# One row of running sums, four weight pieces on GpSimd, and a copied k by transfer, in a fused attention, expert and gated kernel

## The chip, the cores and the metric

The kernel runs on one core of a Trainium2 chip. The metric is device time in microseconds of one execution, the median of the runs shown. Engines: PE (TensorE), DVE (VectorE), ACT (ScalarE), POOL (GpSimd), and SP (SyncE), which only issues DMAs here; ACT issues a few as well.

## What is computed

Shapes: B=2, H=8, S=576, D=64 for the attention; 1152 tokens of width 512, four experts of width 1024, then a gated pair of width 1536. All in float32.

```python
scores = scale * np.matmul(q, k.transpose(0, 1, 3, 2))
cum = np.cumsum(np.maximum(s, 0.0), axis=-1)
bias = -(cum[:, :, :, None] - cum[:, :, None, :])
scores = np.where(causal, -1e9, scores + np.minimum(bias, 0.0))
attn = softmax(scores)                 # sum + 1e-9 below
x = attn @ v                           # to (1152, 512)
for e in range(4):
    out += p[:, e:e+1] * (np.maximum(x @ w1[e], 0.0) @ w2[e])
y = ((out @ w_a) * (out @ w_b)) @ w_out
```

For a row of scores the term -cum of the query is the same in every column and drops out of the softmax; what is left to add is cum of the key. The kernel adds it inside the score matmul, as further rows of k against rows of constants of q.

## The kernel before, in words

Attention is worked off in four groups, (batch, query tiles): group 0 is batch 0, tiles 0 to 1; group 1 is batch 0, tiles 2 to 4; group 2 batch 1, tiles 0 to 2; group 3 batch 1, tiles 3 to 4. In each group the eight heads follow each other. One step is one tile of 128 queries of one head, 80 steps in all. `attn_step` (L786) is a software pipeline over them: at step n it transposes the tile of step n-3 on PE, computes the scores of n (`st_scores`, L586), normalizes the tile of n-2 (`st_norm`), takes the softmax of n-1 (`st_softmax`), evacuates the transposes of n-3 (`st_evac`), and after a head's last tile multiplies with v (`st_av`, L660, tile `av`). At a head's first step the next head's k and q are prepared (`prep_job`, L550) and those of the head after that loaded (`load_job`, L537).

Group 0 is in plain float32. Its q, k and v for all heads (`qa`, `ka`, `va`) are loaded at the start. Its score matmul has 67 rows: 64 of head dimension and three rows with a high, middle and low part of cum minus a value `c0` per row, made in `ckr` and copied into `ka` by three DMAs on ACT's queue (L748). GpSimd multiplies q by the scale first (L554). Groups 1 to 3 split every operand into a high part in the rounded float32 format (F32R) and a low part. Their scores are two matmuls: `ks` (high k, and low k in the other 64 rows) against `qh`, and `kb` (high k again, plus the three rows from the DRAM scratch `ckD`) against `qb`. `kb`'s 64 rows are a second copy of high k, made by GpSimd from the raw `kr` (L566); `ks` is made by ACT (L565) and, for its low half, by GpSimd (L569).

The softmax is a fused operation on DVE that adds the mask to the scores and takes the negated row minimum `mn` (L611), an exponential on ACT with its sum `l` (L623), the addition of 1e-9 on ACT (L628), a reciprocal on DVE (L629) and the multiplication on GpSimd (L630).

The first two experts run beside the attention: between the steps PE gets expert matmuls (L258; 576 of 256 columns each belong to the first part). Their weights come in 16 pieces of 512 KB. A piece is loaded by SP into one of three `raw` buffers (L147) and split by `split_piece` (L190) into `wh` and `wl`: the first eight pieces' high half by GpSimd (L214, two operations of 128x512), later ones by ACT (L218), the low half (L219) by GpSimd for odd pieces and DVE for even ones. Products are three matmuls, high times high, high times low and low times high. The tiles `wh` and `wl` share a pool of four buffers with `qa`, `ka`, `va` and `ckr`.

Each engine takes its instructions in order. That order is made beforehand by a list scheduler that models times, from the program's dependences; only the DMAs inside `in_order` keep the order in which they're written. How far the attention steps are spread between expert products is set by `area`, a running sum of the tile widths, and by `ends`, the step at which a group is complete. So a change of one operation can move others far away.

Of the kernel before, what the change touches and what calls it, by code (L numbers as in the profile page):

```python
# [8 lines left out]
F32 = mybir.dt.float32  # L9
# [3 lines left out]
ALU = mybir.AluOpType  # L13
# [32 lines left out]
NTT = NT // P  # L46
NT0 = 256


@with_exitstack  # L50
def fused_kernel(ctx, tc, qT, kT, v, s, dp, w1, w2, wa, wb, wo, out):
# [138 lines left out]
    def split_piece(r, key, form, wide, src, j):  # L190
# [5 lines left out]
        elif form == "half":  # L196
            split(wh, wl, r, nc.gpsimd)
        elif form == "pair" and wide:
            if j == 0:
                wides[key] = pools["cv"].tile([P, NC, 2 * P], I32, tag="tp", name="tp")  # L200
            t = wides[key]
            narrow(t[:, 2 * j : 2 * j + 2], r[:, :, :, 0], r[:, :, :, 1])
            if j:
                split_pair(key, t.bitcast(F32), nc.gpsimd)
        elif form == "pair":
            split_pair(key, r, nc.vector)
        else:
            nsplit[0] += 1
            first_ones = nsplit[0] <= 8
            lo_eng = nc.gpsimd if nsplit[0] % 2 else nc.vector  # L210
            for m in range(2):
                hi = wh[:, 2 * j + m, :]
                if first_ones:
                    nc.gpsimd.tensor_scalar(  # L214
                        out=hi, in0=r[:, m, :], scalar1=1.0, scalar2=1.0, op0=ALU.mult, op1=ALU.mult
                    )
                elif m == 0:
                    nc.scalar.activation(out=wh[:, 2 * j : 2 * j + 2, :], in_=r, func=AF.Copy)  # L218
                lo_eng.tensor_tensor(  # L219
                    out=wl[:, 2 * j + m, :], in0=r[:, m, :], in1=hi.bitcast(F32), op=ALU.subtract  # L220
                )
# [328 lines left out]
    def prep_job(j):  # L550
        j.t = {}
        if j.gi == 0:
            q = first["q"][:, j.h, :]
            nc.gpsimd.tensor_scalar(  # L554
                out=q[:D], in0=q[:D], scalar1=SCALE, scalar2=1.0, op0=ALU.mult, op1=ALU.mult
            )
            j.qh, j.kr, j.vs = q[:RB], first["k"][:RB, j.h, :], first["v"][:, j.h]
            return
# [45 lines left out]
    def st_softmax(j, i):  # L604
# [132 lines left out]
    )  # L737
    for x in (slice(0, NT0), slice(NT0, S)):
        hi, mid, lo = (y[:, x] for y in ck3)
        d_ = dif[:, x]  # L740
        nc.vector.tensor_scalar(out=d_, in0=cum[:, x], scalar1=c0, scalar2=None, op0=ALU.subtract)
        nc.scalar.activation(out=hi, in_=d_, func=AF.Copy)
        nc.vector.tensor_tensor(out=d_, in0=d_, in1=hi.bitcast(F32), op=ALU.subtract)
        nc.scalar.activation(out=mid, in_=d_, func=AF.Copy)
        nc.vector.tensor_tensor(out=lo, in0=d_, in1=mid.bitcast(F32), op=ALU.subtract)
        if x.start == 0:
            for j_ in range(3):
                in_order(nc.scalar.dma_start(  # L748
                    out=first["k"][D + j_ : D + j_ + 1, :, :], in_=ck3[j_][:H, x].bitcast(F32)
                ))  # L750
# [9 lines left out]
    nc.vector.memset(causal, 0.0)  # L760
    nc.gpsimd.affine_select(
        out=causal[:, S - P :], in_=causal[:, S - P :], pattern=[[-1, P]], compare_op=ALU.is_ge, fill=MASKED,
        base=0, channel_multiplier=1,
    )

# [20 lines left out]
    def attn_step():  # L786
# [365 lines left out]
```

## Time and profile before

| | us |
|---|---|
| median of 3 runs | 768.46 (766.67, 768.46, 769.26) |
| the profiled execution | 768.68 |
| its span, first to last instruction | 766.9 |
| PE busy | 721.4 (94%) |
| DVE busy | 534.2 (70%) |
| ACT busy | 334.4 (44%) |
| POOL busy | 440.0 (57%) |

The mean granted clock of PE over the span is 0.984 of full speed. 58.35 MB are moved by DMA. The attention with the first experts takes the first 240 us, about; the rest is matmuls for the experts and the gated pair. The table's shares are means over the span; the stretches are read apart, in the rows below.

### The profile page before, as it was taken

The numbers are of one execution on the slowest core, as the hardware profiler recorded it, in microseconds if no ns is written. First come the engines' busy times: TensorE is split into PE (matmuls) and PEld (weight loads), VectorE is DVE, ScalarE is ACT, GpSimd is POOL, SyncE is SP. The second block draws the span as 40 slices with busy tenths as digits, with TensorE's granted clock in tenths as the row PEclk, the third lists the DMA queues.
The fourth block names the chain that finished last, engine by engine and source line by source line (L and its number), as shares of the span: only waits on it lengthen the run. The fifth ranks groups of instructions, "written<-read, shape, count | busy, mean of one in ns | idle before, by whom it ended". The sixth has DMA issues, their size and how long they took to land.

```text
span 766.9 us, 11091 instructions
## 1 busy us (share of the span) xinstructions
PE 721.4 (94%) x3868; PEld 628.3 (82%) x3868; DVE 534.2 (70%) x1076; ACT 334.4 (44%) x770; POOL 440.0 (57%) x385
## 2 busy tenths in 40 slices
PE   2889989897997999999999999999899999999998
PEld 2559988885986888888888888898698989878886
DVE  5459675757747987676666557669964788888764
ACT  3558766868844433223213232242635424242410
POOL 4979864657731573443123333678466787898600
PEclk9869999999999999999999999999999999999999
DMA  5435411223302030212011111213111222322003
GB/s 164 154 115 203 158 44 53 79 58 109 95 26 83 27 110 29 77 60 75 9 55 56 56 48 62 83 57 107 31 54 56 83 82 83 97 97 82 3 1 124
DMA packets 33208, 58.35 MB, mean 76 GB/s; under 512 B 3104, under 2 KB 18512, under 8 KB 33152
## 3 DMA queue, kind: packets, MB, share of 16 engines
q1 hardware_dynamic: 32944, 57.48, 23.2%
q8 instruction: 31, 0.51, 0.3%
q14 instruction: 25, 0.20, 0.1%
q10 hardware_dynamic: 208, 0.16, 0.1%
HBM read 55.02 MB, written 2.58 MB: 75 GB/s over the span
## 4 chain that ended last, share of the span: by engine, by line
PE 70%; DVE 14%; POOL 6%; ACT 4%; issue 3%; DMA 2%; ACTq 0%; DVEq 0%; POOLq 0%; SPq 0%
PE ps L258 33%; PE psq L258 22%; PE pst L258 6%; PE av L677 4%; POOL wl L72 3%; PE tr L641 2%; PE sc L601 1%; DVE wl L219 1%; PE sc L599 1%; POOL tp L153 1%; PE sc L602 1%; ACT e L623 1%; DVE e L611 1%; POOL ks L569 1%; DMA kr<-in_kT 1%
## 5 line engine op out<-in xcount | busy, mean ns | idle before, releaser
L258 PE MATMUL ps<-wh,h2h 128*128 128x512 f32 x332 | 131.0, 395 | 2.0 <-DVE acc L304 1.7
L72 POOL TENSOR_TENSOR wl<-raw,wh 128x1024 fp32r<-128x1024 f32 x24 | 58.2, 2435 | 124.5 <-ACT wh L71 94.1
L258 PE MATMUL ps<-wl,h2h 128*128 128x512 f32 x332 | 129.7, 391 | 0.0
L258 PE MATMUL ps<-wh,h2l 128*128 128x512 f32 x332 | 125.7, 392 | 0.0
L306 DVE SCALAR_TENSOR_TENSOR acc<-ps,pr,acc 128x512 f32<-128x512 f32 x111 | 82.0, 745 | 38.5 <-PE ps L258 37.6
L258 PE MATMUL psq<-xh,wh 128*128 128x448 f32 (+1 forms) x224 | 81.6, 366 | 1.7 <-DVE xs L699 1.7
L258 PE MATMUL psq<-xl,wh 128*128 128x448 f32 (+1 forms) x224 | 81.6, 364 | 0.0
L258 PE MATMUL psq<-xh,wl 128*128 128x448 f32 (+1 forms) x224 | 81.5, 364 | 0.0
L258 PEld LDWEIGHTS ps<-wh,h2h 128*128 128x128 f32 x332 | 62.4, 188 | 15.0 <-ACT h2h L317 2.0
L258 PEld LDWEIGHTS ps<-wh,h2l 128*128 128x128 f32 x332 | 62.2, 188 | 13.9 <-DVE h2l L72 0.7
L258 PEld LDWEIGHTS ps<-wl,h2h 128*128 128x128 f32 x332 | 62.4, 188 | 11.0
L317 ACT ACTIVATE h2h<-psq 128x448 fp32r<-128x448 f32 (+1 forms) x56 | 29.4, 530 | 94.7 <-PE psq L258 74.6
L630 POOL TENSOR_SCALAR e<-e,r 128x128 f32<-128x128 f32 (+4 forms) x80 | 47.8, 602 | 31.0 <-DVE r L629 27.4
L72 POOL TENSOR_TENSOR wl<-sums,wh 128x1024 fp32r<-128x1024 f32 x24 | 58.5, 2438 | 6.7 <-ACT wh L71 6.7
L611 DVE CUSTOM_DVE_ANT_0 e<-sc,causal 128x128 f32<-128x128 f32 (+3 forms) x80 | 35.9, 452 | 37.8 <-PE tr L641 28.8
L71 ACT ACTIVATE wh<-raw 128x1024 fp32r<-128x1024 f32 x24 | 25.5, 1061 | 69.9 <-PE ps L258 53.7
L258 PE MATMUL psq<-tqh,wh 128*128 128x448 f32 x144 | 53.0, 368 | 1.5 <-DVE h2l L72 1.4
L258 PE MATMUL psq<-tql,wh 128*128 128x448 f32 x144 | 52.6, 365 | 0.0
L623 ACT ACTIVATE e<-e,mn 128x128 f32<-128x128 f32 (+4 forms) x80 | 45.9, 574 | 15.4 <-DVE mn L611 13.5
L258 PE MATMUL psq<-tqh,wl 128*128 128x448 f32 x144 | 52.4, 364 | 0.0
L656 ACT ACTIVATE eh<-tr 128x512 fp32r<-128x512 f32 (+6 forms) x96 | 38.9, 412 | 27.6 <-PE tr L641 26.7
L153 POOL TENSOR_SCALAR tp<-tp 128x512 f32<-128x512 f32 x24 | 47.2, 1983 | 6.1 <-ACT tp L152 6.1
(170 smaller groups left out, 1974.0 us busy)
## 6 DMA issues: line engine op xcount, KB each, us to landing
raw<-in_w SPq DMA_DIRECT2D x40, 512.0 KB, 3.7
raw<-in_wa SPq DMA_DIRECT2D x12, 512.0 KB, 3.6
raw<-in_wb SPq DMA_DIRECT2D x12, 512.0 KB, 3.6
raw<-in_wo SPq DMA_DIRECT2D x12, 512.0 KB, 3.6
kr<-in_kT SPq DMA_DIRECT2D x16, 288.0 KB
vr<-in_v SPq DMA_DIRECT2D x16, 160.0 KB, 3.3
out<-acc SPq DMA_DIRECT2D x9, 256.0 KB, 2.0
qr<-in_qT SPq DMA_DIRECT2D x8, 192.0 KB, 2.6
```

Of the source, the lines that this page charges most:

```text
L71: nc.scalar.activation(out=hi, in_=src, func=AF.Copy)
L72: lo_eng.tensor_tensor(out=lo, in0=src, in1=hi.bitcast(F32), op=ALU.subtract)
L153: nc.gpsimd.tensor_scalar(out=t.bitcast(F32), in0=t.bitcast(F32), scalar1=2.0**-15, scalar2=GMAX, op0=ALU.max, op1=ALU.min,)
L258: nc.tensor.matmul(ps, lhsT=l, rhs=r, start=first and k == 0, stop=last and k == 2, skip_group_check=more)
L306: nc.vector.scalar_tensor_tensor(out=dst, in0=ps, scalar=share, in1=dst, op0=ALU.mult, op1=ALU.add)
L317: nc.scalar.activation(out=hh, in_=src, func=AF.Relu)
L611: nc.vector.tensor_tensor_reduce(out=t.e[:, c0:c1], in0=ps, in1=causal[:, m0 + c0 : m0 + c1], scale=-1.0, scalar=seed, op0=ALU.add, op1=AL ...
L623: nc.scalar.activation(out=t.e, in_=t.e, func=AF.Exp, bias=mn, scale=-1.0, accum_out=t.l)
L630: nc.gpsimd.tensor_scalar(out=t.e, in0=t.e, scalar1=r, scalar2=1.0, op0=ALU.mult, op1=ALU.mult)
L641: nc.tensor.transpose(ps[:, c - c0, :], t.e[:, k0 : k0 + P], ident)
L656: nc.scalar.activation(out=hi, in_=src, func=AF.Copy)
L677: nc.tensor.matmul(ps[:, o:] if j.gi else ps[a : a + D, o:], lhsT=j.vs[:, c, :], rhs=e[:, c, o:], start=(m == 0), stop=(m == len(mms) - 1),)
```

## The change

Group 0 has one row of sums instead of three. q isn't scaled any more: the row of q that meets the sums holds 1/SCALE = 8, the scores come out 8 times too large, and the scale is put into the exponential (L621) and, by a DVE operation on the minimum (L620), into its bias. The running sum is made in two parts, 256 columns first, and the row goes to `ka` by one DMA right after the first part (L734). The high, middle and low rows for the other groups follow over all 576 columns at once. The mask `causal` is made by GpSimd, earlier. In group 0 the 1e-9 is added and the tile normalized by DVE (L629, L633) instead of ACT and GpSimd. Weight pieces: the first NFIRST = 4 have both halves made by GpSimd, the high half in one operation; later ones have the high half made by ACT and the low half alternating as before. The second copy of k becomes a transfer from `ks` to `kb` on SP's queue (L563). `st_av` is called one step later, ahead of `st_evac`; `ends` and `area` follow.

```diff
-            first_ones = nsplit[0] <= 8
-            lo_eng = nc.gpsimd if nsplit[0] % 2 else nc.vector
...
+            lo_eng = nc.gpsimd if nsplit[0] % 2 or nsplit[0] <= NFIRST else nc.vector
+            two = slice(2 * j, 2 * j + 2)
+            if nsplit[0] <= NFIRST:
+                nc.gpsimd.tensor_scalar(
+                    out=wh[:, two, :], in0=r, scalar1=1.0, scalar2=1.0, op0=ALU.mult, op1=ALU.mult
+                )
+            else:
+                nc.scalar.activation(out=wh[:, two, :], in_=r, func=AF.Copy)
...
         if j.gi == 0:
-            q = first["q"][:, j.h, :]
-            nc.gpsimd.tensor_scalar(
-                out=q[:D], in0=q[:D], scalar1=SCALE, scalar2=1.0, op0=ALU.mult, op1=ALU.mult
-            )
-            j.qh, j.kr, j.vs = q[:RB], first["k"][:RB, j.h, :], first["v"][:, j.h]
+            j.qh, j.kr, j.vs = first["q"][: D + 1, j.h, :], first["k"][: D + 1, j.h, :], first["v"][:, j.h]
...
-        nc.gpsimd.tensor_scalar(
-            out=j.kb[:D], in0=j.kr[:D], scalar1=1.0, scalar2=1.0, op0=ALU.mult, op1=ALU.mult
-        )
+        nc.sync.dma_start(out=j.kb[:D].bitcast(F32), in_=j.ks[:D].bitcast(F32))
...
-        nc.scalar.activation(out=t.e, in_=t.e, func=AF.Exp, bias=mn, scale=-1.0, accum_out=t.l)
+        if j.gi == 0:
+
+            nc.vector.tensor_scalar(out=mn, in0=mn, scalar1=SCALE, scalar2=None, op0=ALU.mult)
+        nc.scalar.activation(
+            out=t.e, in_=t.e, func=AF.Exp, bias=mn, scale=-1.0 if j.gi else -SCALE, accum_out=t.l
+        )
...
-        nc.scalar.activation(out=t.l, in_=t.l, func=AF.Copy, bias=1e-9)
+        if j.gi == 0:
+            nc.vector.tensor_scalar(out=t.l, in0=t.l, scalar1=1e-9, scalar2=None, op0=ALU.add)
+        else:
+            nc.scalar.activation(out=t.l, in_=t.l, func=AF.Copy, bias=1e-9)
         nc.vector.reciprocal(out=r, in_=t.l)
-        nc.gpsimd.tensor_scalar(
+        (nc.gpsimd if j.gi else nc.vector).tensor_scalar(
...
+    half = H // 2
+    nc.vector.memset(first["q"][D : D + 1, :half], 1.0 / SCALE)
+
+    nc.vector.tensor_scalar(out=sc[:, :NT0], in0=sc[:, :NT0], scalar1=0.0, scalar2=None, op0=ALU.max)
+    nc.vector.tensor_tensor_scan(
+        out=cum[:, :NT0], data0=ones[:NR, :NT0], data1=sc[:, :NT0], initial=0.0,
+        op0=ALU.mult, op1=ALU.add,
+    )
+    in_order(nc.scalar.dma_start(out=first["k"][D : D + 1, :, :], in_=cum[:H, :NT0]))
...
-        if x := at(n - 3):
-            st_evac(*x)
+        if x := at(n - 4):
             j, i = x
             if i == j.i1 - 1:
                 st_av(j)
+        if x := at(n - 3):
+            st_evac(*x)
...
-    ends = [max(n for n, (j, i) in enumerate(seq) if j.gi == g) + 4 for g in range(len(GROUPS))]
+    ends = [max(n for n, (j, i) in enumerate(seq) if j.gi == g) + 5 for g in range(len(GROUPS))]
...
-    for n in range(len(seq) + 8):
+    for n in range(len(seq) + 12):
```

Three places show how the order of instructions moves. The first is the start of DVE, up to the scan on which the first score matmul waits; `s_sb` holds s, `va` the tile that also holds the sums. Before:

```order
L756 MEMSET qa 3x2048
L722 MEMSET ones 128x576
L758 MEMSET qb_83 3x384
L758 MEMSET qb_84 3x384
L760 MEMSET causal 128x576
L730 TENSOR_SCALAR s_sb<-s_sb 32x576
L731 SCALAR_TENSOR_TENSOR va<-ones,s_sb 32x576
```

Now:

```order
L727 MEMSET qa 1x1024
L725 MEMSET ones 128x576
L742 MEMSET qa 1x1024
L770 MEMSET qb_83 3x384
L770 MEMSET qb_84 3x384
L729 TENSOR_SCALAR s_sb<-s_sb 32x256
L750 TENSOR_SCALAR s_sb<-s_sb 32x320
L730 SCALAR_TENSOR_TENSOR va<-ones,s_sb 32x256
```

The memset of three rows of q became two of one row, that of `causal` left DVE, and the scan comes in a part of 256 columns, behind both halves of the max.

The second is SP's queue where the weights of pieces 4 to 9 are issued (`raw`; names of the others go on with the head, the group's first tile and a number, so `kb_2_2` belongs to head 2 of group 1, whose tiles begin at 2). Before:

```order
L546 DMA qr_1_2_446<-in_qT 128x384
L147 DMA raw<-in_w 128x1024 x2
L546 DMA qr_2_2_503<-in_qT 128x384
L547 DMA kr_1_2_447<-in_kT 128x576
L576 DMA vr_1_2_531<-in_v 128x320
L147 DMA raw<-in_w 128x1024 x2
L548 DMA kb_2_2_505<-ckD 3x576
L547 DMA kr_2_2_504<-in_kT 128x576
L546 DMA qr_3_2_602<-in_qT 128x384
L576 DMA vr_2_2_633<-in_v 128x320
L147 DMA raw<-in_w 128x1024 x2
```

Now:

```order
L149 DMA raw<-in_w 128x1024
L547 DMA qr_1_2_442<-in_qT 128x384
L563 DMA kb_0_2_391<-ks_0_2_435 64x576
L149 DMA raw<-in_w 128x1024
L547 DMA qr_2_2_500<-in_qT 128x384
L548 DMA kr_1_2_443<-in_kT 128x576
L571 DMA vr_1_2_526<-in_v 128x320
L549 DMA kb_2_2_502<-ckD 3x576
L149 DMA raw<-in_w 128x1024
L563 DMA kb_1_2_444<-ks_1_2_493 64x576
L547 DMA qr_3_2_578<-in_qT 128x384
L149 DMA raw<-in_w 128x1024 x3
```

The loads of k's three rows for head 2 (`kb_2_2<-ckD`) stood behind pieces 6 and 7 and now stand ahead of piece 6; the copies `kb<-ks` of heads 0 and 1 are new.

The third is PE at the first scores of head 1 of group 1 (`sc_1_2`, then the tile and a number; L258, now L259, are expert matmuls into `ps`). Before:

```order
L258 MATMUL ps_635<-xl,wh 128x256
L258 MATMUL ps_635<-xh,wl 128x256
L258 MATMUL ps_671<-xl,wh 128x256
L258 MATMUL ps_671<-xh,wl 128x256
L601 MATMUL sc_1_2_2_612<-ks_1_2_496,qh_1_2_445 128x320
L602 MATMUL sc_1_2_2_612<-kb_1_2_448,qb_83 128x320
L677 MATMUL av_6_0_525<-eh_6_0_486,va 64x256
L677 MATMUL av_6_0_525<-eh_6_0_486,va 64x128
L601 MATMUL sc_1_2_3_657<-ks_1_2_496,qh_1_2_445 128x448
L602 MATMUL sc_1_2_3_657<-kb_1_2_448,qb_83 128x448
L641 MATMUL tr_7_0_0_533<-ident,e_7_0_0_481 128x128
```

Now:

```order
L259 MATMUL ps_802<-xh,wl 128x256
L259 MATMUL ps_845<-xh,wl 128x256
L259 MATMUL ps_924<-xh,wl 128x256
L259 MATMUL ps_924<-xh,wh 128x256
L259 MATMUL ps_924<-xl,wh 128x256
L259 MATMUL ps_924<-xh,wl 128x256
L596 MATMUL sc_1_2_2_588<-ks_1_2_493,qh_1_2_441 128x320
L597 MATMUL sc_1_2_2_588<-kb_1_2_444,qb_83 128x320
L596 MATMUL sc_1_2_3_637<-ks_1_2_493,qh_1_2_441 128x448
L597 MATMUL sc_1_2_3_637<-kb_1_2_444,qb_83 128x448
```

What stood after 27 expert matmuls and ahead of the last `av` of group 0 now stands after 84 of them and behind that `av`. Counted over the whole order, 68 expert matmuls stood ahead of the end of the `av` of head 0 of group 1, and now 140; from the end of the `av` of head 4 of group 1 to that of head 1 of group 2 there were 101, and now 18. Near the attention's end, in heads 5 and 6 of group 3, the next head's transposes now stand ahead of the `av`, where they stood behind it.

## Rows read from the trace of the kernel before

**Rows 1.** The page: PE's granted clock in 40 slices.

```profile
PEclk9869999999999999999999999999999999999999
```

**Rows 2.** Waits of PE, 0 to 60 us: engine, line, releaser, total us, times, longest.

```profile
PE sc L599 <- DMA ka<-ckr: 13.4, 1, 13.4
```

**Rows 3.** Chain that ended last, 0 to 16 us: start, length, what.

```profile
1.29 1.76 DVE qa L756
...
5.72 1.36 DVE va L731
...
9.23 0.88 ACTq L748
...
10.97 2.15 DMA ka<-ckr
...
13.42 1.64 PE sc L599 x4
```

**Rows 4.** Timeline of DVE at the start: start, length, engine, line, operation.

```profile
3.24 0.54 DVE L722 MEMSET ones<- 128x576 f32 x1 [0.18 <-issue]
...
3.89 0.78 DVE L758 MEMSET qb<- 3x384 f32 x2
...
5.30 0.38 DVE L730 TENSOR_SCALAR s_sb<-s_sb 32x576 f32<-32x576 f32 x1
...
7.41 0.84 DVE L741 TENSOR_SCALAR dif<-va,c 32x256 f32<-32x256 f32 x2
```

**Rows 5.** Windows of the first group: us, busy PE, PEld, DVE, ACT, POOL; PEclk.

```profile
20.00:30.00 10.00, 9.28 (x37) 5.87 (x35) 5.70 (x15) 6.12 (x24) 9.92 (x17) 1.00 0.45 153
30.00:40.00 10.00, 7.18 (x26) 5.09 (x26) 4.95 (x18) 5.08 (x18) 9.90 (x15) 0.65 0.35 117
...
33.00:48.00 15.00, 13.31 (x42) 8.56 (x42) 5.14 (x18) 6.62 (x25) 14.33 (x20) 0.50 0.25 93
```

**Rows 6.** Windows of three other stretches, same columns.

```profile
52.00:60.00 8.00, 6.17 (x40) 4.98 (x40) 6.37 (x19) 6.53 (x21) 5.20 (x7) 1.00 0.61 200
130.00:135.00 5.00, 4.00 (x32) 3.47 (x30) 3.49 (x13) 4.52 (x16) 4.28 (x8) 1.00 0.26 75
130.00:145.00 15.00, 12.45 (x88) 10.44 (x87) 11.52 (x47) 13.84 (x53) 11.90 (x22) 1.00 0.31 90
```

**Rows 7.** Window at the end of the attention, same columns.

```profile
220.00:240.00 20.00, 14.17 (x90) 11.62 (x89) 10.39 (x26) 9.46 (x24) 4.40 (x6) 1.00 0.07 21
```

**Rows 8.** DVE by form, 18 to 36 us: line, operation, shapes, count, total, mean ns.

```profile
L629 DVE RECIPROCAL r<-l 128x1 f32<-128x1 f32 x10 | 1.4, 155 | 2.7 <-ACT l L628 2.7
```

**Rows 9.** Timeline of DVE beside GpSimd's weight pieces.

```profile
18.41 0.58 DVE L771 TENSOR_SCALAR den<-den 128x9 f32<-128x9 f32 x1 [0.86 <-POOL den L770]
19.38 0.19 DVE L772 RECIPROCAL den<-den 128x9 f32<-128x9 f32 x1
...
26.98 2.01 DVE L219 TENSOR_TENSOR wl<-raw,wh 128x512 fp32r<-128x512 f32 x2
...
42.99 0.42 DVE L611 CUSTOM_DVE_ANT_0 e<-sc,causal 128x256 f32<-128x256 f32 x1 [1.91 <-PE tr L641]
```

**Rows 10.** Chain of the wait for k, 180 to 194 us.

```profile
184.18 3.04 DMA kr<-in_kT
...
187.37 0.61 POOL kb L566
```

**Rows 11.** Chain of two heads near the attention's end.

```profile
228.14 1.16 PE av L677 x8
229.30 0.47 PE tr L641 x4
...
231.28 0.49 ACT eh L656
...
231.80 0.70 DVE el L658
...
232.55 1.16 PE av L677 x8
```

More of the change, by code (lines that the diff above doesn't have):

```diff
@@ L47 @@
 NT0 = 256
+NFIRST = 4
 @with_exitstack
@@ L208, in split_piece @@
             nsplit[0] += 1
-            first_ones = nsplit[0] <= 8
-            lo_eng = nc.gpsimd if nsplit[0] % 2 else nc.vector
-            for m in range(2):
-                hi = wh[:, 2 * j + m, :]
-                if first_ones:
-                    nc.gpsimd.tensor_scalar(
-                        out=hi, in0=r[:, m, :], scalar1=1.0, scalar2=1.0, op0=ALU.mult, op1=ALU.mult
-                    )
-                elif m == 0:
-                    nc.scalar.activation(out=wh[:, 2 * j : 2 * j + 2, :], in_=r, func=AF.Copy)
+            lo_eng = nc.gpsimd if nsplit[0] % 2 or nsplit[0] <= NFIRST else nc.vector
[6 more added lines that the diff above has]
+                nc.scalar.activation(out=wh[:, two, :], in_=r, func=AF.Copy)
+            for m in (2 * j, 2 * j + 1):
                 lo_eng.tensor_tensor(
-                    out=wl[:, 2 * j + m, :], in0=r[:, m, :], in1=hi.bitcast(F32), op=ALU.subtract
+                    out=wl[:, m, :], in0=r[:, m - 2 * j, :], in1=wh[:, m, :].bitcast(F32), op=ALU.subtract
                 )
@@ L565, in prep_job @@
         nc.scalar.activation(out=j.ks, in_=j.kr, func=AF.Copy)
-        nc.gpsimd.tensor_scalar(
-            out=j.kb[:D], in0=j.kr[:D], scalar1=1.0, scalar2=1.0, op0=ALU.mult, op1=ALU.mult
-        )
+        nc.sync.dma_start(out=j.kb[:D].bitcast(F32), in_=j.ks[:D].bitcast(F32))
         nc.gpsimd.tensor_tensor(
@@ L722, in fused_kernel @@
     nc.vector.memset(ones, 1.0)
+    half = H // 2
[6 more added lines that the diff above has]
+    in_order(nc.scalar.dma_start(out=first["k"][D : D + 1, :, :], in_=cum[:H, :NT0]))
+    nc.gpsimd.memset(causal, 0.0)
+    nc.gpsimd.affine_select(
+        out=causal[:, S - P :], in_=causal[:, S - P :], pattern=[[-1, P]], compare_op=ALU.is_ge, fill=MASKED,
+        base=0, channel_multiplier=1,
+    )
+    make_identity(nc, ident)
+    nc.vector.memset(first["q"][D : D + 1, half:], 1.0 / SCALE)
     nc.gpsimd.memset(pick, 1.0)
@@ L729, in fused_kernel @@
         )
-    nc.vector.tensor_scalar(out=sc, in0=sc, scalar1=0.0, scalar2=None, op0=ALU.max)
+    nc.vector.tensor_scalar(out=sc[:, NT0:], in0=sc[:, NT0:], scalar1=0.0, scalar2=None, op0=ALU.max)
     nc.vector.tensor_tensor_scan(
-        out=cum, data0=ones[:NR], data1=sc, initial=0.0, op0=ALU.mult, op1=ALU.add
+        out=cum[:, NT0:], data0=ones[:NR, NT0:], data1=sc[:, NT0:], initial=cum[:, NT0 - 1 : NT0],
+        op0=ALU.mult, op1=ALU.add,
     )
@@ L737, in fused_kernel @@
     )
[L738 to L750, printed above, removed]
+    hi, mid, lo = ck3
+    nc.vector.tensor_scalar(out=dif, in0=cum, scalar1=c0, scalar2=None, op0=ALU.subtract)
+    nc.scalar.activation(out=hi, in_=dif, func=AF.Copy)
+    nc.vector.tensor_tensor(out=dif, in0=dif, in1=hi.bitcast(F32), op=ALU.subtract)
+    nc.scalar.activation(out=mid, in_=dif, func=AF.Copy)
+    nc.vector.tensor_tensor(out=lo, in0=dif, in1=mid.bitcast(F32), op=ALU.subtract)
     for j_ in range(3):
@@ L754, in fused_kernel @@
         ))
-    make_identity(nc, ident)
-    nc.vector.memset(first["q"][D:RB], 1.0)
     for qb in qbs:
         nc.vector.memset(qb[D:].bitcast(F32), 1.0)
[L760 to L764, printed above, removed]
     nc.sync.dma_start(out=pr, in_=dp)
```

1 line of the change is left out of this document (removed).

## The prediction

> **What bounds the kernel now.** I read the page first: the granted clock of PE is at nine tenths or more in 38 of 40 slices, with a dip in the second and third [rows 1]. The run that was profiled took 768.68 us, 0.22 above the median of 768.46; the sum below starts from 768.68. From about 60 us PE is busy nearly all the time, apart from the attention's last third, so the change can only gain where PE stands still. I then looked for those places with PE's waits and with windows. The largest is the start: PE waits 13.4 us, once, for the rows of sums in `ka` [rows 2]. The chain shows how these come about: a memset, the scan, two differences and roundings, the issue of a DMA on ACT's queue, 2.15 us until it lands, then the first scores at 13.42 [rows 3]. The second is 52 to 60 us, where PE is busy 6.17 of 8.00 us [rows 6]. The third are heads with few expert products between their steps: 12.45 of 15.00 us busy, and 4.00 of 5.00 in the emptiest part [rows 6]. The last is the attention's end, 14.17 of 20.00 [rows 7].
>
> **The start: minus 4.2 us.** Three roundings, two subtractions and two of three issues leave the path; the first scores need one scan of 256 columns. DVE begins at 1.29 [rows 3]. It now does two memsets of 1024 columns, half of the 1.76 each [rows 3], and those of `ones` (0.54) and `qb` (0.78) [rows 4]: 0.88 + 0.54 + 0.88 + 0.78 = 3.08. With some 0.4 of gaps, as between the same rows before, that ends at 4.8. Both halves of the max stand ahead of the scan; one of 576 columns took 0.38 [rows 4], and I put 0.5 for two. The scan of 256 takes 256/576 of 1.36, so 0.60. That is 5.9. One issue (0.88) and the landing (2.15) follow [rows 3], then 0.30 from the landing to the first matmul (13.42 less 10.97 and 2.15). The sum is 9.2 instead of 13.42. q's scaling on GpSimd leaves too; it was ahead of its need. The memset of `causal` moves from DVE to GpSimd, which is idle then.
>
> **DVE in the first group: 0, and up to plus 14.3.** Each of 16 steps gives DVE three operations that other engines did or that weren't there: 32 of one column (the minimum times SCALE, the sum plus 1e-9) and 16 that norm a tile. The one-column reciprocal has a mean of 0.155 [rows 8], so 32 x 0.155 = 5.0; a norm costs at most what the subtraction of `dif` costs, 0.84 for two [rows 4], so 16 x 0.42 = 6.7. Away go the low halves of pieces 2 and 4, about 2.0 us each [rows 9]: plus 7.7 in all. DVE was busy 5.70 and 4.95 of 10 us [rows 5], and the group lasts from 13.42 to the last of its tiles at 42.99 [rows 9], so of these 30 us DVE had 9.35 / 20 x 30 = 14.0 free. 6.3 stay free, and PE, which is the busier one there, hides the work. What isn't known is whether DVE is held up by GpSimd, which is busy 9.92 of 10 us with weights [rows 5]. The nearest row says it can be: `den`, nine columns, took 0.58 [rows 9] where a one-column operation takes 0.155, so 0.43 more; its reciprocal, a moment later, took 0.19 [rows 9]. All 48 held like that are 20.6 us, 14.3 more than the room. I take none, since ten reciprocals in the same stretch were not held [rows 8], and keep both ends. The Trainium skill has a rule that speaks against this change: in "SBUF — State Buffer", section "Who interferes with whom", a DVE tensor_scalar may take the port pair that it shares with GpSimd, and then whoever comes second is blocked for the other's whole instruction. By that rule norms and the new one-source operations could all be held, and the sum would be that of the first rival below; the reciprocal isn't on its list, and the trace agrees with both, with one row for each.
>
> **Weights and the lead at 45 to 60 us: minus 1.8.** GpSimd loses 16 norms, 8 scalings of q and four high halves to others, and gives its time to pieces 1 to 4. With the first group done earlier, PE's order has 140 expert matmuls ahead of the end of the next head's `av`, where it had 68. They fill what is idle between 52 and 60, 8.00 - 6.17 = 1.83 [rows 6]. Against that, SP issues the sixth piece only behind `kb_2_2`, which waits for PE's scores of head 0, where it used to issue two pieces ahead of it; so piece 6 is late if anything is. And ACT now does the high halves of pieces 5 to 8, ahead of softmax steps. The bounds are minus 1.8 and, if two pieces come late by a low half of 2.0 each [rows 9], plus 4.0.
>
> **Heads with little expert work: plus 2.6.** The products put forward are missing later. From the `av` of head 4 in the second group to that of head 1 in the third, the order had 101 expert matmuls and now has 18. Three more heads have next to nothing between their steps; such a head takes 4.4 us, from one `av` at 228.14 to the next at 232.55 [rows 11], so three take 13.2. At the emptiest rate, 1.00 idle of 5.00 [rows 6], that is 13.2 / 5 x 1.00 = 2.6. The bounds are 2.2 by the 15-us row (2.55 / 15 x 13.2) [rows 6] and 3.8 by the end of the attention (5.83 / 20 x 13.2) [rows 7].
>
> **The copy of k: minus 0.6.** 24 copies leave GpSimd and become 24 transfers on SP's queue. Most are hidden on either side, as k is prepared a head ahead. In the wait for k, GpSimd's 0.61 stands behind a transfer of `kr` [rows 10]; that one goes. The new transfer starts once ACT has made `ks`, and takes at least the 2.15 of the small one [rows 3] and about the 3.04 of `kr` [rows 10]; a head lasts 4.4 us [rows 11], so it is hidden. Queued behind it on SP are the next `qr`, `kr` and a weight piece, each by the issue of one DMA; bounds minus 1.2 and plus 1.
>
> **av a step later: minus 2.2.** Near the end a head runs as transposes 0.47, evacuation 0.49, low part 0.70, `av` 1.16, one after the other [rows 11]. The changed order puts the next head's transposes ahead of this `av` for two heads, so that `av` runs beside the evacuation: 2 x 1.1. The bounds are 0, if evacuation sets the pace, and minus 2.3.
>
> **The sum**: 768.68 - 4.2 - 1.8 + 2.6 - 0.6 - 2.2 = 762.5. Its own range is 760 to 767: down, what the last three terms still allow (0.4, 0.6 and 0.1, with as much for the start); up, the two largest bounds that don't hang together, 2.2 for `av` and some of the weights' 5.8, not all of it.
>
> **Rivals.** *DVE is held in the first group* (slower). If three quarters of the 48 operations wait as `den` did, 36 x 0.43 = 15.5, less the 6.3 of room, 9.2 come on top: 771.7. All 48 give 776.8. The room is used up at 15 held operations, and from 29 on the kernel is slower than before, (6.2 + 6.3) / 0.43. For it: `den` [rows 9]. Against it: ten reciprocals that weren't held [rows 8]; GpSimd begins on weights only behind DVE's `den`, half-way through the group, and PE isn't waiting for DVE then. 0.17. *The gain is given back*: the sixth piece comes late, so the lead costs half of a low half, 1.0, instead of giving 1.8, heads without expert work cost 3.8 and `av` gives nothing: 768.68 - 4.2 + 1.0 + 3.8 - 0.6 = 768.7, no change. For it: SP's order, and the emptiness of [rows 7]. 0.22. *The clock*: from 33 to 48 us PE was granted 0.50, half of 2.4 GHz, and was busy 13.31 of 15 [rows 5]. If such a stretch lasts half as long again, 7.5 x 0.5 x 13.31 / 15 = 3.3 come on top: 765.8. 0.08. If there is no such stretch, up to 13.31 / 2 = 6.7 go: 755.8. Nothing on the page says which; what preceded the fall was a stretch with PE busy 9.28 of 10 us [rows 5]. 0.10. *The row of sums isn't the start's bound*, as q or k of head 0 come later: they are the first in their queues, and the wait was for `ka<-ckr` alone [rows 2], so I give that nothing of its own.
>
> **How the numbers follow.** The forecast has 0.43. A measurement tells 0.3%, about 2.3 us, from no change: faster is below 766.2, slower above 770.8. Faster: 0.41 of the forecast, both clock cases 0.18, less 0.01 = 0.58. Same: 0.02 of the forecast, 0.19 of the given-back case, 0.02 of the first rival = 0.23. Slower: 0.15 of the first rival, 0.03 of the second and 0.01 of the clock's = 0.19. The range goes from 755.5 to 772: it takes in the clock's gain and the first rival's price, and leaves out its far end.
>
> **What would show it.** In the changed profile the first score matmul should start near 9.2 us, and PE's wait for `ka` be that long. DVE's one-column operations near 0.16 in the first group would speak for the sum; near 0.5, or a norm over 1 us beside a row of GpSimd's weights, for the first rival. 52 to 60 us should be full, and the windows around the seventh head of the second group emptier than 4.00 of 5.00. A wait of PE for `wh` before 60 us, or SP waiting long for PE's scores, would mean the second rival. The prediction is wrong if the start gains 4 us and the kernel doesn't.

## The result and the profile after

| | before | changed |
|---|---|---|
| median of 4 runs, us | 768.72 | 757.5 |
| all runs, us | 766.67 to 769.26 | 756.23 to 760.76 |
| ratio, 95% interval | | 0.9867 (0.9842 to 0.9893) |
| profiled execution, span, us | 768.68, 766.9 | 760.76, 759.0 |

The changed kernel is faster by 1.3%, 11.2 us by the medians. The forecast was 762.5, in a range of 755.5 to 772. The direction was right and the gain was almost twice the 6.2 that the sum gave. The profiled execution of the changed kernel is the slowest of its four, so its trace shows 7.9 us of the gain.

The changed kernel's page, PE's busy tenths and granted clock in 40 slices, which answers to [rows 1]:

```profile
PE   5979897997998999999999999999899999999997
...
PEclk9999998999998999999999999999999999999999
```

Its waits of PE from 0 to 60 us, which answer to [rows 2]:

```profile
PE sc L594 <- DMA ka<-va: 8.9, 1, 8.9
PE ps L259 <- DVE hl L287: 3.2, 2, 2.7
```

Its timeline at the start, which answers to [rows 3, 4]:

```profile
5.15 0.67 DVE L730 TENSOR_TENSOR_SCAN va<-ones,s_sb 32x256 f32<-32x256 f32 x1
...
5.86 1.24 ACTq L734 DMA_DIRECT2D ka<-va  x1
...
8.94 1.62 PE L594 MATMUL sc<-ka,qa 65*128 65x128 f32 x4 [8.94 <-DMA ka<-va]
```

The scan ends at 5.8, where the sum had 5.9, and the first scores come at 8.94 instead of 13.42. Its windows in the stretches of [rows 5 to 7] (us, busy time of PE, PEld, DVE, ACT, POOL, then PE's clock):

```profile
20.00:30.00 10.00, 10.00 (x47) 7.25 (x45) 6.27 (x35) 5.81 (x20) 9.12 (x9) 1.00 0.32 100
30.00:40.00 10.00, 8.57 (x50) 6.01 (x48) 6.88 (x23) 7.08 (x22) 5.64 (x6) 1.00 0.38 121
33.00:48.00 15.00, 12.40 (x74) 10.60 (x75) 9.56 (x25) 9.94 (x25) 10.44 (x10) 0.89 0.43 138
52.00:60.00 8.00, 5.32 (x31) 4.73 (x32) 6.99 (x18) 8.00 (x20) 5.01 (x4) 1.00 0.78 272
130.00:145.00 15.00, 13.03 (x82) 11.70 (x83) 12.10 (x45) 12.99 (x51) 8.35 (x15) 0.89 0.33 93
```

Between 33 and 48 us PE was granted 0.89 instead of 0.50, and it worked off 74 matmuls there instead of 42. From 52 to 60 it is emptier than before, not full. The last `av` of the attention ends at 229.9 instead of 237.9: all 8 us of this execution's gain lie in the attention. To that point PE's idle time fell from 33.8 to 29.2 us, which is the start's 4.5 and nothing else, and its busy time from 204.1 to 200.7, for the same 1248 matmuls. This second part goes with the clock: up to the last `av` PE was granted half for 20.5 us before and for 10.2 now. Behind it the changed kernel has more of such time than before, 10.2 us against 3.4, so over the whole span the difference is small, 23.9 against 20.4.

### The profile page after: what moved, and what is told of

Same layout as the page of the kernel before. It is cut to its first block, busy times and chain, and to the rows that moved or that the text cites. A ratio compares the mean times of both kernels' runs of the same rounds, so it can differ in the third digit from the quotient of the medians.

```text
span 759.0 us, 11106 instructions
## 1 busy us (share of the span) xinstructions
PE 719.9 (95%) x3868; PEld 630.9 (83%) x3868; DVE 533.0 (70%) x1119; ACT 334.8 (44%) x756; POOL 416.2 (55%) x330
## 4 chain that ended last, share of the span: by engine, by line
PE 55%; DVE 12%; POOL 8%; issue 4%; ACT 2%; DMA 1%; POOLq 0%; ACTq 0%; DVEq 0%; SPq 0%
PE ps L259 27%; PE psq L259 20%; PE pst L259 4%; POOL wl L74 3%; PE av L680 2%; POOL tp L155 1%; DVE tp L167 1%; PE tr L644 1%; DVE tp L163 1%; DVE h2l L74 1%; DVE acc L1027 1%; DVE tp L159 1%; POOL t L155 1%; DVE t L167 1%; DVE psq L405 1%
## 5 line engine op out<-in xcount | busy, mean ns | idle before, releaser
L259 PE MATMUL ps<-wh,h2h 128*128 128x512 f32 x332 | 130.6, 393 | 0.0
L259 PE MATMUL ps<-wl,h2h 128*128 128x512 f32 x332 | 129.6, 390 | 0.0
L259 PE MATMUL ps<-wh,h2l 128*128 128x512 f32 x332 | 125.7, 392 | 0.8 <-DVE h2l L74 0.8
L259 PE MATMUL psq<-xh,wh 128*128 128x448 f32 (+1 forms) x224 | 82.9, 372 | 1.7 <-DVE xs L702 1.7
L259 PE MATMUL psq<-xl,wh 128*128 128x448 f32 (+1 forms) x224 | 82.6, 369 | 0.0
L259 PE MATMUL psq<-xh,wl 128*128 128x448 f32 (+1 forms) x224 | 82.6, 370 | 0.0
L259 PEld LDWEIGHTS ps<-wh,h2l 128*128 128x128 f32 x332 | 62.2, 188 | 14.7 <-DVE h2l L74 1.6
L259 PEld LDWEIGHTS ps<-wh,h2h 128*128 128x128 f32 x332 | 62.4, 188 | 11.8 <-ACT h2h L73 0.3
L259 PEld LDWEIGHTS ps<-wl,h2h 128*128 128x128 f32 x332 | 62.4, 188 | 11.1
L633 POOL TENSOR_SCALAR e<-e,r 128x448 f32<-128x448 f32 (+4 forms) x64 | 39.9, 630 | 28.9 <-DVE r L632 27.5
L259 PE MATMUL psq<-tqh,wh 128*128 128x448 f32 x144 | 52.9, 368 | 0.9 <-DVE h2l L74 0.5
L259 PE MATMUL psq<-tql,wh 128*128 128x448 f32 x144 | 52.6, 365 | 0.0
L259 PE MATMUL psq<-tqh,wl 128*128 128x448 f32 x144 | 52.5, 364 | 0.0
L621 ACT ACTIVATE e<-e,mn 128x128 f32<-128x128 f32 (+4 forms) x80 | 45.9, 574 | 11.6 <-DVE mn L606 9.1
L644 PE MATMUL tr<-ident,e 128*128 128x128 f32 x240 | 45.2, 291 | 6.1 <-DVE el L661 4.1
```

What stands on the lines that cost most here:

```text
L259: nc.tensor.matmul(ps, lhsT=l, rhs=r, start=first and k == 0, stop=last and k == 2, skip_group_check=more)
L633: (nc.gpsimd if j.gi else nc.vector).tensor_scalar(out=t.e, in0=t.e, scalar1=r, scalar2=1.0, op0=ALU.mult, op1=ALU.mult)
L644: nc.tensor.transpose(ps[:, c - c0, :], t.e[:, k0 : k0 + P], ident)
```

## The experiments

Three further columns are read from each run's trace: the start of the first score matmul, PE's idle time over the span (the span less PE's busy time), and the time at half rate. The last is worked out from windows of 2 us up to PE's last matmul, which ends some 4 us before the span does; each window counts with twice what its granted clock lacks to 1. In the row of the kernel before, these columns are of its first profile.

| run | median, us | ratio to before, 95% | first | idle | half rate | span |
|---|---|---|---|---|---|---|
| before | 769 | | 13.42 | 45.5 | 23.9 | 766.9 |
| changed, first profile | 757.5 | 0.9867 (0.9842 to 0.9893) | 8.94 | 39.1 | 20.4 | 759.0 |
| same_again | 759.8 | 0.9877 (0.9853 to 0.9901) | 8.71 | 40.5 | 10.2 | 756.6 |
| late_start | 761.14 | 0.9893 (0.9871 to 0.9916) | 13.35 | 43.2 | 13.6 | 761.0 |
| start_alone | 766.35 | 0.9959 (0.9942 to 0.9976) | 8.85 | 41.5 | 27.3 | 765.3 |
| norm_back | 764.93 | 0.9944 (0.9924 to 0.9964) | 8.82 | 39.5 | 34.1 | 762.7 |
| norm_mul_back | 763.11 | 0.9915 (0.9896 to 0.9935) | 8.66 | 42.9 | 20.4 | 762.0 |
| kcopy_back | 768.76 | 0.9975 (0.9958 to 0.9993) | 8.62 | 42.5 | 27.3 | 766.1 |
| av_back | 766.21 | 0.9950 (0.9931 to 0.9969) | 8.69 | 40.9 | 30.7 | 766.7 |
| pieces_back | 755.81 | 0.9808 (0.9789 to 0.9828) | 8.76 | 34.6 | 17.0 | 754.5 |
| pieces_lo | 757.6 | 0.9851 (0.9828 to 0.9875) | 8.88 | 39.4 | 17.0 | 755.9 |
| pieces_hi8 | 757.71 | 0.9848 (0.9823 to 0.9874) | 8.56 | 37.4 | 20.4 | 756.1 |
| kcopy_pieces_back | 760.48 | 0.9888 (0.9860 to 0.9916) | 8.87 | 38.8 | 20.4 | 756.8 |
| av_pieces_back | 756.98 | 0.9837 (0.9816 to 0.9859) | 8.86 | 35.9 | 17.2 | 755.6 |

The runs were made in three lots, each beside runs of the kernel before on the same chip (medians 769.0, 769.8 and 769.4), so the ratios are what is compared, and a difference of ratios times 769 gives us. In every row, span less idle less half of the time at half rate is 706 to 711 us, while the spans lie 12.4 us apart: these two make up most of what the executions differ in, and leave up to 5 us open.

**same_again.** No edit.

> The changed kernel once more, unaltered, beside the kernel before. Its profiled execution had three stretches at 1.2 GHz after the start (43 to 46, 118 to 122 with 131 to 135, and 230 to 237 us), and four executions spread from 756.2 to 760.8. Theory A (the gain is what the order of the work gives: 4.5 us at the start and the rest from fewer idle places): about 757.5 again, and another profile has the same idle times of PE. Theory B (part of the gain is less time at 1.2 GHz, and that varies from execution to execution): the time moves with the clock's mean, about 2 us for each 4 us at half rate.

759.8, with 0.9877 again inside the first interval. The two profiles of the one kernel have nearly the same idle time, 39.1 and 40.5, and 20.4 and 10.2 us at half rate; half of that difference, 5.1, less the 1.4 of idle time, is 3.7, and their spans differ by 2.4. Theory B holds for these two. Over more executions the tie is loose: of the 17 of the kernel before in this lot the slowest, 772.45, had the lowest mean clock, 0.977, but one of 770.49 had the highest, 0.987. And by the mean clock it isn't most of the change's gain: the mean over the ten executions of the changed kernel is 0.985, over these 17 it is 0.983, which is some 2 us of 767.

**late_start.**

```diff
-    in_order(nc.scalar.dma_start(out=first["k"][D : D + 1, :, :], in_=cum[:H, :NT0]))
...
     nc.vector.tensor_tensor(out=lo, in0=dif, in1=mid.bitcast(F32), op=ALU.subtract)
+    nc.vector.scalar_tensor_tensor(
+        out=dif[:H, :NT0], in0=lo[:H, :NT0].bitcast(F32), scalar=0.0, in1=cum[:H, :NT0],
+        op0=ALU.mult, op1=ALU.add,
+    )
+    in_order(nc.scalar.dma_start(out=first["k"][D : D + 1, :, :], in_=dif[:H, :NT0]))
```

> The changed kernel with the row of sums sent to ka only after all three parts of the sums are made, by one further DVE operation, so the first score matmul starts near 14 us instead of 8.9; the rest as changed. Theory A (the start is worth what it moves): 5 us slower than the changed kernel, 762 to 763. Theory B (the stretch from the first matmul to 26 us runs at half rate in either kernel, so work put there is worth half, unless the clock then stays up): 2.5 us slower, 760, if the stretch at 1.2 GHz after 33 us stays short; 766 or more if it comes back to 17 us.

The first scores came 4.6 us later than in same_again, and the kernel was 1.2 us slower by the ratios, with intervals that overlap; they allow up to some 3.8, so A's 5 us are excluded, and B's 2.5 are not. Idle time other than the wait for the start fell from 20.1 to 16.0 us up to the last `av`, which ended at 227.7 against 228.1: what was started early waited later. Part of that is weights: the early start didn't bring them earlier, as SP issued the sixth piece at 39.9 us in the changed kernel and at 34.8 here. In the changed kernel's profile ACT waits 3.9 us for a `raw` piece between 48 and 52 us; in late_start all its waits for pieces from 26 to 60 us add up to 1.0.

**start_alone.** The diff's parts on the normalization, the weight pieces, the copy and the place of `av` are undone, and the start with one row is left.

> The early start with one row of sums alone: normalization, weight pieces, the copy of k and the place of av are as in the kernel before. Theory A: 4 us faster than before, 764 to 765. Theory B: the stretch at 1.2 GHz decides; if it is as long as before, 2 to 3 us faster, 766; if short, 760.

0.9959, some 3 us faster than before; A and B were a us apart and the interval (1.8 to 4.5 us) takes in both; B's 760 for a short stretch at 1.2 GHz didn't apply, as it was 10.2 us from 26 to 60. With the first scores 4.6 us earlier, the last `av` ended 3.1 earlier.

**norm_back.**

```diff
-        if j.gi == 0:
-            nc.vector.tensor_scalar(out=t.l, in0=t.l, scalar1=1e-9, scalar2=None, op0=ALU.add)
-        else:
-            nc.scalar.activation(out=t.l, in_=t.l, func=AF.Copy, bias=1e-9)
+        nc.scalar.activation(out=t.l, in_=t.l, func=AF.Copy, bias=1e-9)
...
-        (nc.gpsimd if j.gi else nc.vector).tensor_scalar(
+        nc.gpsimd.tensor_scalar(
```

> The changed kernel with group 0's addition of 1e-9 back on ACT and its normalization back on GpSimd. If DVE held up by GpSimd had cost something, this is faster; after the trace, in which the one-column operations took 0.14 to 0.16, it is not. Theory A: GpSimd is again late with weights and each normalization waits behind a piece, so 2 to 4 us slower, 760 to 761. Theory B: the pace of the first group falls with it, PE has gaps from 28 to 36 us, and the stretch at 1.2 GHz is long again: 5 us slower or more, 762 to 765.

0.9944: the normalization on DVE is worth 5.2 us (0.0067 x 769). Theory B's number came. GpSimd's timeline shows the queue, three tiles of group 0 behind the two operations of a weight piece's low half:

```profile
31.57 2.82 POOL L220 TENSOR_TENSOR wl<-raw,wh 128x512 fp32r<-128x512 f32 x2
34.37 1.18 POOL L630 TENSOR_SCALAR e<-e,r 128x128 f32<-128x128 f32 x3
```

PE's waits from 26 to 60 us, and then ACT's timeline, show a longer way that the loss took:

```profile
PE tr L641 <- ACT eh L656: 5.0, 1, 5.0
PE av L677 <- ACT eh L656: 2.3, 2, 1.8
```

```profile
38.17 1.06 ACT L218 ACTIVATE wh<-raw 128x1024 fp32r<-128x1024 f32 x1 [4.12 <-DMA raw<-in_w]
```

PE's wait of 5.0 us, from 36.1 to 41.1, is for ACT's evacuation of the transposes. ACT came to it only at 40.7, as it had stood 4.1 us, until 38.2, for the load of a weight piece, whose high half is ahead of the evacuation in its queue. SP issued that load, the fifth, at 32.5 us instead of the changed kernel's 28.6. PE was idle 8.9 us from 26 to 60 against 7.0 in same_again, and 13.7 against 3.4 us at half rate.

**norm_mul_back.** Only the second hunk of norm_back.

> The changed kernel with only the multiplication of group 0's normalization back on GpSimd; the addition of 1e-9 stays on DVE. With both back the kernel was 5 us slower. Theory A (GpSimd's queue: a tile waits there behind weight pieces of 1.2 us): all of it is the multiplication, 764 to 765 again, with PE idle about 9 us from 26 to 60. Theory B (ACT: 16 additions of 0.2 us lengthen each step's chain): the multiplication is worth little, 760 to 761.

0.9915, 2.9 us slower than same_again by the ratios, between the two theories: PE's idle time from 26 to 60 was 10.8 us, the most of all runs, but its time at half rate only 6.8. Here too one wait of PE is 5.1 us long, for an evacuation by ACT, and ACT stood 3.6 us for a weight piece. That the addition on ACT is worth the other 2.3 is not shown; this run's interval overlaps with both norm_back's and same_again's.

**pieces_back.** `split_piece` as before.

> The changed kernel with the weight pieces split as before: eight high halves by GpSimd in two operations each, low halves alternating from the first piece. Theory A (all gain is idle time of PE): GpSimd has 9 us more of high halves and DVE 4 us more of low halves before 60 us, weights come later, 1 to 3 us slower than the changed kernel, 761 to 763. Theory B (what an edit of the first 60 us is worth is how long PE runs at 1.2 GHz there, 3.4 us in the changed kernel and 13.7 with the normalization back): 4 to 6 us slower if gaps of PE between 28 and 45 us come back, none if they don't.

Neither: 0.9808, 5.3 us *faster* than the changed kernel, and the fastest of all. The new splitting takes back 5.3 of the 14.8 us that the rest gains. From 26 to 60 us PE was busy almost throughout at full clock, where same_again had 27.04; the window of pieces_back and then that of same_again:

```profile
26.00:60.00 34.00, 32.17 (x213) 26.98 (x212) 27.70 (x86) 21.83 (x67) 31.84 (x30) 1.00 0.58 186
```

```profile
26.00:60.00 34.00, 27.04 (x167) 22.16 (x166) 24.21 (x70) 23.46 (x62) 25.01 (x21) 0.95 0.57 179
```

GpSimd is the busier one in the faster kernel: 31.84 of 34 us against 25.01. In the first profile of the changed kernel GpSimd did nothing from 33.8 to 38.1 us, with four high halves and three low halves made; what it waited for isn't settled, as the profile names a load of v, and ACT's high half of the fifth piece ended at 38.0 as well. What the trace does show is how PE's longest gap between 26 and 60 us, 52.0 to 54.7, comes about. ACT stands for a late piece, whose high half is now ACT's; behind it stand the evacuation of an expert product (L286), its low part on DVE (L287, also behind the piece's low half) and PE. From the timelines of ACT, DVE and PE:

```profile
51.91 1.06 ACT L218 ACTIVATE wh<-raw 128x1024 fp32r<-128x1024 f32 x1 [3.94 <-DMA raw<-in_w]
52.88 0.92 ACT L286 ACTIVATE hh<-ps 128x256 fp32r<-128x256 f32 x3
...
54.21 0.42 DVE L287 SCALAR_TENSOR_TENSOR hl<-ps,hh 128x256 fp32r<-128x256 f32 x1
...
54.69 0.38 PE L259 MATMUL ps<-xh,wh 128*128 128x256 f32 x1 [2.72 <-DVE hl L287]
```

In pieces_back no gap of PE from 26 to 60 us is longer than 0.7, though ACT waits 3.7 us for pieces there too, 2.1 at most in one wait. That this chain is the whole 5.3 is not shown.

**pieces_lo and pieces_hi8.** One half of that edit each:

```diff
-            lo_eng = nc.gpsimd if nsplit[0] % 2 or nsplit[0] <= NFIRST else nc.vector
+            lo_eng = nc.gpsimd if nsplit[0] % 2 else nc.vector
```

> The changed kernel with the low halves alternating between GpSimd and DVE from the first piece, as before; the high halves as changed (four by GpSimd in one operation each, later ones by ACT). With the whole splitting as before the kernel was 5 us faster than the changed one. Theory A (four pieces wholly on GpSimd make a queue of 15 us there, and the weights come too late for expert products that stand early in PE's order): the 5 us are here, 755 to 757. Theory B (high halves on ACT, which stand ahead of the exponentials and evacuations in ACT's order): this run stays near 760.

```diff
-            if nsplit[0] <= NFIRST:
+            if nsplit[0] <= 8:
```

> The changed kernel with the high halves of the first eight pieces by GpSimd instead of four; low halves of the first four by GpSimd as changed. Theory A (GpSimd's queue is too long): slower than the changed kernel, 762 to 765, since it adds 4 x 1.2 us there. Theory B (ACT's high halves are what cost): faster, 755 to 757.

0.9851 and 0.9848: each some 2 us faster than the changed kernel, within the intervals, and neither has all of the 5. A's slowing in pieces_hi8 didn't come, so GpSimd's queue in itself wasn't too long. ACT's waits for weight pieces from 26 to 60 us add up to 2.5 us in pieces_lo and to nothing in pieces_hi8, against 6.6 and 7.0 in the changed kernel. Time at half rate there doesn't account for either run: it was 10.2 and 6.8 us, more than the changed kernel's 3.4. How the loss is shared between the two halves stays open.

**kcopy_back and kcopy_pieces_back.** The copy of k on GpSimd, in the changed kernel and with the pieces as before:

```diff
-        nc.sync.dma_start(out=j.kb[:D].bitcast(F32), in_=j.ks[:D].bitcast(F32))
+        nc.gpsimd.tensor_scalar(
+            out=j.kb[:D], in0=j.kr[:D], scalar1=1.0, scalar2=1.0, op0=ALU.mult, op1=ALU.mult
+        )
```

> The changed kernel with the second copy of k made by GpSimd again. Theory A: GpSimd has 0.5 to 0.7 us more per head, one wait for k in 180 to 194 us grows by 0.6, so 0 to 1 us slower, 760 to 761. Theory B: no change of the clock's stretches, as the copy isn't in the first group, apart from two copies before 45 us; 760. A rival: the transfers on SP's queue delay weights, and without them it is 1 to 3 us faster, 757 to 759.

> The fastest so far (weight pieces as before) with the second copy of k back on GpSimd. In the changed kernel that copy's return cost 7 us. Theory A (GpSimd's time and its queue matter: 24 copies of 0.5 to 0.7 us, two of them before 45 us, stand ahead of norms and low halves): 4 to 8 us slower than 755.8, 760 to 764, with more waits of PE for evacuations and low parts after 60 us. Theory B (most of the 7 us was time at 1.2 GHz that follows gaps of PE in the first 60 us, and these gaps came from the weights): with the pieces as before the copy costs 0 to 2 us, 756 to 758.

0.9975 against 0.9877, and 0.9888 against 0.9808: the transfer is worth 7.5 and 6.2 us, in both without overlap of the intervals. Theory A holds in the second run, and all three expectations of the first were too low. For the second pair a reason shows in the chain of kcopy_pieces_back from 177 to 186 us, where there is one buffer for `kr`, and the next load waits until GpSimd has read it twice, with tiles to normalize in between:

```profile
177.67 0.62 POOL e L636
...
179.42 0.66 POOL kb L564
180.08 0.73 POOL e L636
...
180.89 1.43 POOL ks L567
...
182.34 2.86 DMA kr<-in_kT
...
185.28 0.69 ACT ks L563
```

In pieces_back the chain between 172 and 182 us has no GpSimd operation:

```profile
173.30 0.74 DVE qb L559
...
174.06 2.27 DMA qr<-in_qT
176.33 0.67 ACT ks L563
```

PE's idle time from 125 to 196 us is 8.4 with the copy on GpSimd and 5.0 without (71.00 less 62.64 and 66.02). In the first pair it is 7.9 with the copy on GpSimd and 8.2 and 8.1 without, so there this loop doesn't explain the 7.5. What differs in that pair is time at half rate, 27.3 us against 20.4 and 10.2; why it came is open.

**av_back and av_pieces_back.** `st_av` at n-3 behind `st_evac`, `+ 4` and `+ 8` as before.

> The changed kernel with the product with v at step n-3 again, behind the evacuation, and the spacing as before. The prediction's term was 2.2 us in the last heads: 762. PE's idle time from 196 us to the attention's end was 1.6 and 2.0 us in the changed kernel and 4.0 before; theory A says it returns to about 4. Theory B: same, unless the first group's order changes; its time at 1.2 GHz from 26 to 60 us stays 3.4.

> The fastest so far with the product with v at step n-3 again. In the changed kernel its return cost 5.6 us, of which the idle time of PE explains about 1.5 and time at 1.2 GHz the rest. Theory A (a fixed worth of the place of av, 80 steps long): 4 to 6 us slower than 755.8, 760 to 762. Theory B (the worth is 1.5 us of idle time, and the clock's part varies with the order): 757 to 759.

0.9950 against 0.9877, 5.6 us, more than the 762 expected allows; with the pieces as before 0.9837 against 0.9808, 2.2 us, with intervals that overlap. PE's idle time from 196 us to the last `av` went from 2.0 to 3.4, and from 2.3 to 3.8. So 1.5 us are that wait. What more there is in the first pair goes with time at half rate, 30.7 us against 20.4 and 10.2 in the changed kernel's two profiles, which the second pair doesn't repeat (17.2 against 17.0); that it is the cause is not shown. Theory B holds in the second.

## Why the prediction was right, and where its sizes were off

**The start** did what its steps said, 9.2 forecast and 8.94 measured, but minus 4.2 was mis-sized as a gain: alone it is some 3, in an interval that takes in 4.2, and taken out of the changed kernel 1.2, in one that doesn't. The step that failed is that time saved ahead of a queue is saved at its end. Against late_start the weights didn't come earlier.

**DVE in the first group: 0** was right in that no cost of it shows, and the first rival's price did not come. DVE by form from 9 to 36 us of the changed kernel:

```profile
L633 DVE TENSOR_SCALAR e<-e,r 128x256 f32<-128x256 f32 x8 | 3.9, 494 | 0.1
L633 DVE TENSOR_SCALAR e<-e,r 128x128 f32<-128x128 f32 x8 | 3.6, 450 | 0.1
...
L629 DVE TENSOR_SCALAR l<-l 128x1 f32<-128x1 f32 x16 | 2.3, 145 | 1.0 <-ACT e L621 0.8
L620 DVE TENSOR_SCALAR mn<-mn 128x1 f32<-128x1 f32 x16 | 2.3, 147 | 0.1
```

The 32 one-column operations took 0.145 and 0.147 on average, as the reciprocal in [rows 8]; `den`'s 0.58 in [rows 9] was no price for them. Of the 16 tiles four were held by GpSimd's work on weights; DVE's timeline, and then GpSimd's at the last two:

```profile
22.05 0.68 DVE L633 TENSOR_SCALAR e<-e,r 128x128 f32<-128x128 f32 x1
...
24.13 0.68 DVE L633 TENSOR_SCALAR e<-e,r 128x256 f32<-128x256 f32 x1
...
30.40 1.17 DVE L633 TENSOR_SCALAR e<-e,r 128x128 f32<-128x128 f32 x1
...
31.67 1.19 DVE L633 TENSOR_SCALAR e<-e,r 128x256 f32<-128x256 f32 x1
```

```profile
30.20 2.51 POOL L220 TENSOR_TENSOR wl<-raw,wh 128x512 fp32r<-128x512 f32 x2
```

The other tiles took 0.27 to 0.36. The 2.51 are two operations of 1.28, and each held tile ended 0.1 to 0.2 us after the GpSimd operation in which it began. The rule of the Trainium skill ("SBUF — State Buffer", "Who interferes with whom") thus agrees for tiles, and the one-column operations show no sign of it: 14 of the 32 began during a GpSimd operation, and none took over 0.16. So the rival's mechanism was there, but few operations met it: they were held for some 2.5 us in all, and the prediction had 6.3 of room. What the term left out is the other side: what the normalization costs on GpSimd, behind weights. That was 5.2 us.

**Weights, minus 1.8:** the sign was wrong. The expert matmuls put forward (140) didn't fill 52 to 60 us: PE stood still from 52.0 to 54.7 us, behind the 3.9 us for which ACT waited for a `raw` piece. The bound of plus 4 and the second rival had the late piece, and the prediction named ACT's high halves ahead of softmax steps, but gave them no price; pieces_back measures the whole splitting with 5.3.

**Heads with little expert work, plus 2.6:** not seen. From 60 us to the last `av` PE was idle 14.6 us before and 14.6 and 13.1 in the two profiles of the changed kernel. Emptier heads around 116 to 135 us were there, but the copy's and `av`'s gains lie in the same stretch, and I can't part them.

**The copy, minus 0.6:** the largest miss, 6 to 7.5 us. The step took one 0.61 out of one wait. With the pieces as before, the chain shows what it left out: the loop has `kr`'s only buffer in it, and in it GpSimd's copy, the tiles ahead of it and the low half follow each other; 3.4 of the 6.2 us are idle time of PE in the stretch with that chain. In the changed kernel the 7.5 aren't idle time there, and their cause stays open.

**av, minus 2.2:** 2.2 measured with the pieces as before, in intervals that overlap, and 5.6 in the changed kernel. The idle time that the term is about, from 196 us to the last `av`, fell from 4.3 us before to 2.0, as forecast.

**The clock.** The rival in which the stretch at 1.2 GHz goes was given 0.10 and 755.8. That stretch went, for the greater part: 17.1 us at half rate between 26 and 60 us before, 3.4 in both profiles of the changed kernel, though part of it came back in later stretches. So the forecast's sum and this rival are not alternatives, as I had them. The prediction also read the fall wrongly: it named a stretch with PE busy 9.28 of 10 us ahead of it, but PE fell between 32 and 34 us, right behind two waits for DVE:

```profile
30.98 1.04 PE L599 MATMUL sc<-ka,qa 67*128 67x128 f32 x4 [1.34 <-DVE mn L611]
...
32.74 0.66 PE L599 MATMUL sc<-ka,qa 67*128 67x128 f32 x2 [0.50 <-DVE mn L611]
```

Taken out one at a time, the five parts are worth 1.2 + 5.2 + 7.5 + 5.6 - 5.3 = 14.2 us against 9.5 for the whole, by the ratios of their lots. They don't add; the order is made anew for each kernel, and time at half rate differs with it. That the time fell well inside the range is in part luck: the copy's miss of 6 to 7 us and the splitting's of some 7 nearly cancel, and the normalization's 5.2 stood in no term.

## What to carry to other kernels

Where one engine splits weights and also stands in a short loop (here norm, copy, low half, and one buffer for k), price an operation that is taken off it by the loop and by its queue, and not by its duration alone. An operation that waits for a load holds up all that stands behind it in its engine's queue: ACT's high halves stood 3.6 to 4.1 us for late pieces in three of these kernels, with PE's evacuations behind them. Where a planner makes the order, measure every edit of a bundle by itself: here the best kernel, 755.8 us, is the changed one without one of its parts. An early start is worth only what the next scarce thing lets through; here weights were part of that.

## What was not expected of the hardware

PE's falls to 1.2 GHz follow gaps, but not every gap has one. In the changed kernel's first profile:

```profile
40.00:42.00 2.00, 0.97 (x6) 0.77 (x6) 1.52 (x7) 1.96 (x8) 1.95 (x3) 1.00 0.53 192
42.00:44.00 2.00, 1.68 (x10) 1.68 (x11) 1.00 (x4) 0.96 (x4) 2.00 (x2) 0.77 1.01 286
44.00:46.00 2.00, 2.00 (x11) 2.00 (x11) 1.42 (x1) 0.94 (x2) 1.84 (x3) 0.50 0.60 220
...
52.00:54.00 2.00, 0.00 (x0) 0.00 (x0) 1.00 (x2) 2.00 (x5) 0.00 (x0) 1.00 0.82 310
54.00:56.00 2.00, 1.31 (x11) 1.32 (x12) 2.00 (x7) 2.00 (x5) 1.19 (x1) 1.00 0.31 92
```

and in that of same_again, the same kernel, around the later gap:

```profile
52.00:54.00 2.00, 0.00 (x0) 0.00 (x0) 1.46 (x3) 2.00 (x5) 0.00 (x0) 1.00 0.51 192
54.00:56.00 2.00, 1.78 (x12) 1.78 (x13) 2.00 (x8) 2.00 (x6) 1.65 (x2) 0.80 0.54 164
56.00:58.00 2.00, 2.00 (x9) 1.81 (x9) 1.99 (x7) 2.00 (x7) 1.92 (x2) 0.50 1.03 395
```

The later gap is not quite the same in both: 2.72 us in the first, without a fall, and 3.25 in same_again, with one. Length alone doesn't decide, as a gap of 2.4 us in pieces_hi8 is followed by a fall. The earlier gap is the clean case, the same matmul behind the same wait; the first profile's has a fall behind it and same_again's, the second line, has none:

```profile
40.89 0.38 PE L259 MATMUL ps<-xl,wh 128*128 128x256 f32 x1 [1.03 <-DVE xl L74]
```

```profile
40.24 0.38 PE L259 MATMUL ps<-xl,wh 128*128 128x256 f32 x1 [1.02 <-DVE xl L74]
```

What decides is left open. Single executions of one kernel differ by several us, with this in part, so single profiles of such kernels are weak evidence for a difference of 2.

Also, the granted clock doesn't show the first stretch. The four matmuls of an `av` of group 0 in the changed kernel:

```profile
19.71 1.54 PE L680 MATMUL av<-eh,va 128*64 128x256 f32 x4
24.36 1.54 PE L680 MATMUL av<-eh,va 128*64 128x256 f32 x4
27.59 0.86 PE L680 MATMUL av<-eh,va 128*64 128x256 f32 x4
```

The first two take almost twice the third's time while the column has 1.00. In the kernel before the change-over lies between 24.64 and 28.78 too, though its PE began 4.5 us later; in late_start, which began at 13.35, it lies between 29.62 and 33.83. In pieces_lo, which began at 8.88, the `av` at 19.64 already took 0.86. So this first stretch has no fixed end. Against the kernel before, work that was moved ahead of it ran at half the rate, which can be a further reason why the early start was worth less than its 4.5 us; late_start, whose first stretch is no shorter, doesn't bear it out.
